# Another column order, a shorter first softmax and a guard with a second path, in a dynamic convolution followed by a maxout layer

## The chip, the cores and the metric

One Trainium2 chip; the kernel runs on one of its cores. The metric is the device time of one execution in microseconds. Engines are named as in the profile: PE is TensorE, DVE VectorE, ACT ScalarE, POOL GpSimd, SP SyncE (it only issues DMAs and waits).

## The reference, cut to what matters

```python
# x: 8 x 4160 x 192, weight_gen: 8 x 4160 x 8 heads x 7 taps, all float32
w = exp(weight_gen - max(weight_gen, axis=-1))
w = w / (sum(w, axis=-1) + 1e-9)            # softmax over the 7 taps
x_pad = concatenate([zeros(B, 6, D), x], axis=1)
# y[b, s, h, g] = sum over k of w[b, s, h, k] * x_pad[b, s + k, h, g]
y = einsum('bshk,bskhg->bshg', w, x_unf).reshape(B * S, 192)
out = maximum(y @ w1, y @ w2) @ w_out       # w1, w2: 192 x 1024, w_out: 1024 x 192
```

`weight_gen` is drawn as a normal variable times 0.3.

## The kernel before, in words

The 33280 tokens lie on 128 partitions, 260 consecutive tokens ("columns", `CPP`) on each; 16 partitions make one of the 8 sequences. A column needs the 6 columns ahead of it (`PAD`), the halo. For column 0 of a partition these are the last columns of the partition before it, or zeros where a sequence begins: `msk` is 0 on those partitions and 1 elsewhere.

The columns are worked through in batches of 16 (`BATCHES`, the seventeenth has 4). For each batch:

- `load_wg` and `load_x` load the logits (`wg_t`) and x (`xb_t`, cast to bf16 by the DMA). The halo of every batch but the first is copied from the tail of the batch before, SBUF to SBUF (`load_halo`).
- The softmax has no maximum: `exp_sum` (ACT) makes the exponentials, `red` (DVE) their sums over the taps, `ln` (ACT) the logarithm of the sums, `shift` (DVE) subtracts it from the logits, and `weights` (ACT) takes the exponential again, as bf16 and with every value twice.
- `mul` (DVE) multiplies seven shifted views of x by the weights into `m_t`; `adds` (DVE) sum the taps into `y_t`, which is transposed by DMA (`yt`, SP's queue; a one-element cast on POOL, `gate`, marks the landing). For the first units of 4 columns `sum_transpose` does sum and transpose on PE into `yps`, and ACT copies that to `yt`.

The second layer uses max(h1, h2) = h1 + relu(h2 - h1). PE multiplies `yt` with `wd` = w2 - w1 into `hd` or `hdp`, ACT applies relu into `rd_t`, PE multiplies that with `wo` = w_out, and adds `yt` times `w10` = w1 w_out, all into `op_ps`. ACT copies this to `o_t`, and SP stores it. `hidden(g)` records the work on group g of these tiles.

The order is the program's own: each engine runs its instructions in the order in which the kernel records them, and `behind(a, b)` makes a load of POOL's queue wait for an instruction. Before the first tiles there is a setup, recorded once:

- SP issues, in this order: logits of batch 0 (`load_wg`), the halo from DRAM in two pieces (partitions 1 to 15 and 16 to 127, 504 KB for the larger), columns 0 to 3 (`xs`), the weights in float32 (`ws0E`, `ws1E`: rows 0 to 127 of w1 and w2, the half 0 of their columns; `ws0T`, `ws1T`: rows 128 to 191 of both halves), columns 4 to 7, half 1 of `ws0E` and `ws1E`, logits of batch 1.
- The first softmax is done in two halves, ahead of everything else on DVE and ACT; the masked halo is cast by DVE (L568) and ACT (L570); `mul(0, 0)` follows.
- `w_diff(h)` forms half h of `wd` by subtraction on DVE and copies parts of it between partition halves (L586, L587, L591), half 0 by ACT, half 1 by DVE. `w1E`, `w1T` are bf16 copies of w1.
- `keep_warm` runs matmuls whose result nobody reads.

The end is one ACT copy into `o_last` (L383), two stores of half of it by SP and ACT (L386), and the waits for the last DMAs.

Of the kernel before, what the change touches and what calls it, by code (L numbers as in the profile page):

```python
# [23 lines left out]
def kernel(  # L24
# [20 lines left out]
    RPB = P // B  # L45
    G = D // H
# [29 lines left out]
    pwg = ctx.enter_context(tc.tile_pool(name="pwg", bufs=4))  # L76
    pxb = ctx.enter_context(tc.tile_pool(name="pxb", bufs=2))
    pe_ = ctx.enter_context(tc.tile_pool(name="pe", bufs=2))
    psm = ctx.enter_context(tc.tile_pool(name="psm", bufs=3))
    pm = ctx.enter_context(tc.tile_pool(name="pm", bufs=1))  # L80
    pen = ctx.enter_context(tc.tile_pool(name="pen", bufs=2))
    py = ctx.enter_context(tc.tile_pool(name="py", bufs=2))
    pyt = ctx.enter_context(tc.tile_pool(name="pyt", bufs=6))
    prd = ctx.enter_context(tc.tile_pool(name="prd", bufs=7))
    first_ps = ctx.enter_context(ExitStack())
# [3 lines left out]
    def later_ps():  # L89

        first_ps.close()
        for k in ("ab", "c", "r"):
            ps[k] = ctx.enter_context(tc.tile_pool(name="pps_" + k, bufs=1, space=bass.MemoryType.PSUM))
# [7 lines left out]
    def load_wg(b, eng):  # L101
        c0, n = BATCHES[b]
        wg_ts[b] = pwg.tile([P, n * WGC], FP32, name="wg_t", tag="wg")
        return eng.dma_start(
            out=wg_ts[b],
            in_=bass.AP(tensor=weight_gen.tensor, offset=c0 * WGC,
                        ap=[[CPP * WGC, P], [1, n * WGC]]),
        )

    def load_x(b, o, n, halo=True):  # L110

        if b not in xb_ts:
            xb_ts[b] = pxb.tile([P, (16 + PAD) * D], BF16, name="xb_t", tag="xb")
        load = nc.gpsimd.dma_start(  # L114
            out=xb_ts[b][:, (PAD + o) * D:(PAD + o + n) * D],
            in_=bass.AP(tensor=x.tensor, offset=(BATCHES[b][0] + o) * D,
                        ap=[[CPP * D, P], [1, n * D]]),
        )
        if b > 0 and o == 0 and halo:
            load_halo(b)  # L120
        return load

    def load_halo(b):

        if b not in xb_ts:
            xb_ts[b] = pxb.tile([P, (16 + PAD) * D], BF16, name="xb_t", tag="xb")
        nc.gpsimd.dma_start(out=xb_ts[b][:, 0:PAD * D],
# [14 lines left out]

    def red(b, i=0, of=1):
        if i == 0:
            s_ts[b] = psm.tile([P, BATCHES[b][1] * H], FP32, name="sum_t", tag="sum")
        hs, at, ap = part(b, i, of)
        nc.vector.reduce_sum(out=s_ts[b][:, hs], in_=_sub(e_ts[b], at, ap), axis=AX.X)  # L147

    def ln(b, i=0, of=1):
        s_t = s_ts[b][:, part(b, i, of)[0]]  # L150
        nc.scalar.activation(out=s_t, in_=s_t, func=AF.Ln)
# [7 lines left out]
    def weights(b, o):  # L159
# [6 lines left out]
        for j in range(J):  # L166
            nc.scalar.activation(  # L167
                out=_sub(en_ts[b], (o * WGC + j * N * K) * 2, [[2 * N, K], [2, N], [1, 2]]),
                in_=_sub(wg_ts[b], (o * H + j * N) * K, [[1, K], [K, N], [0, 2]]), func=AF.Exp,
            )  # L170


    def mul(b, o):

        n = dict(pieces(b))[o]
        if n == 4 and b < 2:
            m_out = _sub(m_t, K * o * D, [[64, 2], [P, K * 6], [1, 64]])
            x_in = _sub(xb_ts[b], o * D, [[2 * D, 2], [D, K], [1, 2 * D]])
        else:
            m_out = m_t[:, K * o * D:K * (o + n) * D]  # L180
            x_in = _sub(xb_ts[b], o * D, [[D, K], [1, n * D]])
# [195 lines left out]
    def evac(p, n):  # L377
# [3 lines left out]
        if p == NT // 2 - 1:  # L381
# [3 lines left out]
            for j, eng in enumerate((nc.scalar, nc.sync)):  # L385
                eng.dma_start(  # L386
                    out=bass.AP(tensor=out.tensor, offset=(place(p)[0] + 2 * j) * D, ap=[[CPP * D, P], [1, D]]),
# [18 lines left out]
        for eng, c, *ap in stores:  # L406

            def issue(eng=eng, c=c, ap=ap, o=o):
                eng.dma_start(
                    out=bass.AP(tensor=out.tensor, offset=c * D, ap=[[CPP * D, P], *ap]),  # L410
# [101 lines left out]
    o_last = consts.tile([P, 2 * D], FP32, name="o_last")  # L512

    with tc.tile_pool(name="pstage", bufs=1) as pstage:
        ident_f = pstage.tile([P, P], FP32, name="ident_f")
        xs = pstage.tile([P, (PAD + 8) * D], FP32, name="xs")
# [3 lines left out]
        load_wg(0, nc.sync)  # L520
        nc.vector.memset(xs[0:1, 0:PAD * D], 0.0)
# [314 lines left out]
```

## Time and profile before

| | |
|---|---|
| runs | 409.07, 409.61, 409.11 us; median 409.11 |
| profiled execution | span 408.4 us, its only time; no other of that execution is given |
| PE busy | 398.9 us, 98% |
| DVE busy | 371.7 us, 91%; nothing after 378.5 us |
| ACT busy | 357.1 us, 87% |
| POOL busy | 72.5 us, 18% |
| granted TensorE clock | 1.000 |
| DMA | 65.70 MB, 161 GB/s over the span |

The span runs from the first instruction to the last of the core; the time of a run also holds what lies around it. Busy time is an average over three stages: loads (until about 14 us), a stretch in which ACT fills and PE starts (to 31 us), and the long stretch to 405 us. A wait is put down to the last semaphore that came.

### The profile page before, as it was taken

To read this page: it belongs to the slowest core of one execution; us is meant where nothing else is said; L and a number is where in the kernel's file an instruction comes from. 1 tells how busy PE (TensorE), PEld (TensorE's weight loads), DVE (VectorE), ACT (ScalarE), POOL (GpSimd) and SP (SyncE) were. 2 spreads that over 40 slices of the span, in tenths; PEclk is the share of its full clock that TensorE was granted. 3 is DMA by queue.
4 is the path that set the end of the run, shared out by engine and by line. 5 is a ranking of instruction groups with operands and counts; after the bars stand their busy time and mean duration, and the time that the engine had idled before them with its cause. 6 is when DMAs were issued, how large, how long until landed. Compare 5 with 4: busy or idle time off the path is not lost.

```text
span 408.4 us, 16153 instructions
## 1 busy us (share of the span) xinstructions
PE 398.9 (98%) x7422; PEld 317.6 (78%) x7422; DVE 371.7 (91%) x216; ACT 357.1 (87%) x424; POOL 72.5 (18%) x101
## 2 busy tenths in 40 slices
PE   7899999999999999999999999999999999999996
PEld 2589989777777777777877777777778777777796
DVE  4999999999999999999999999999999999999000
ACT  6799899999899998898998999998999988988872
POOL 0311012212222112121211122220122220210000
PEclk9999999999999999999999999999999999999999
DMA  8958399767658674976786588478648647654514
GB/s 242 218 125 219 75 186 167 168 165 173 147 113 237 151 167 105 244 201 69 234 203 84 123 248 202 65 243 180 128 109 239 169 68 237 154 127 111 145 55 142
DMA packets 62785, 65.70 MB, mean 161 GB/s; under 512 B 47711, under 2 KB 51679, under 8 KB 62718
## 3 DMA queue, kind: packets, MB, share of 16 engines
q1 hardware_dynamic: 54334, 40.54, 36.7%
q0 software_dynamic: 8240, 24.04, 29.9%
q8 instruction: 58, 0.95, 1.0%
q10 hardware_dynamic: 144, 0.10, 0.1%
q14 instruction: 9, 0.07, 0.1%
HBM read 35.96 MB, written 25.56 MB: 151 GB/s over the span
## 4 chain that ended last, share of the span: by engine, by line
PE 91%; ACT 4%; DMA 3%; issue 1%; SPq 0%; DVE 0%; ACTq 0%
PE op_ps L339 41%; PE hd L299 39%; PE op_ps L351 8%; DMA xs<-in_x_dram 3%; ACT rd_t L309 2%; PE hdp L299 1%; PE yps L248 1%; ACT yt L255 1%; ACT w1t L675 0%; ACT e_t L135 0%; ACT en_t L167 0%; DVE xb_t L620 0%; ACT wd L591 0%; ACT w L668 0%; ACT w1T L633 0%
## 5 line engine op out<-in xcount | busy, mean ns | idle before, releaser
L309 ACT ACTIVATE rd_t<-hd 128x1024 bf16<-128x1024 f32 (+1 forms) x206 | 234.7, 1187 | 27.5 <-PE hd L299 26.3
L339 PE MATMUL op_ps<-wo,rd_t 64*128 64x192 bf16 x4160 | 211.4, 243 | 0.1
L339 PEld LDWEIGHTS <-rd_t 64*128 64x128 bf16 x4160 | 181.7, 94 | 15.7 <-ACTq L372 0.3
L299 PE MATMUL hd<-yt,wd 64*128 64x512 bf16 (+1 forms) x1584 | 188.1, 360 | 0.7 <-issue 0.6
L182 DVE TENSOR_TENSOR m_t<-xb_t,en_t 128x10752 bf16<-128x10752 bf16 (+1 forms) x37 | 187.4, 5070 | 0.2
L299 PEld LDWEIGHTS <-wd 64*128 64x128 bf16 x1776 | 94.5, 94 | 43.2 <-issue 2.8
L224 POOL CAST gate<-yt 128x1 f32<-128x1 bf16 x29 | 37.8, 1305 | 264.3 <-DMA yt<-y_t 264.3
L198 DVE TENSOR_TENSOR m_t<-m_t 128x4608 bf16<-128x4608 bf16 (+1 forms) x30 | 74.1, 2470 | 0.1
L395 ACT COPY o_t<-op_ps 128x384 f32<-128x384 f32 (+1 forms) x99 | 57.3, 589 | 12.8 <-PE op_ps L339 12.8
L351 PE MATMUL op_ps<-w,yt 64*128 64x192 bf16 x780 | 56.0, 243 | 0.4 <-ACT w L668 0.4
L351 PEld LDWEIGHTS <-yt 64*128 64x128 bf16 x780 | 38.6, 94 | 16.7 <-issue 1.3
L204 DVE TENSOR_TENSOR m_t<-m_t 128x3072 bf16<-128x3072 bf16 (+1 forms) x29 | 50.0, 1723 | 0.1
L167 ACT ACTIVATE en_t<-wg_t 128x896 bf16<-128x896 f32 (+2 forms) x45 | 35.8, 821 | 0.0
L207 DVE TENSOR_TENSOR y_t<-m_t 128x1536 bf16<-128x1536 bf16 (+1 forms) x29 | 27.3, 941 | 0.5
L114 POOL DMA_DIRECT2D xb_t<-in_x_dram x33 | 17.6, 534 | 32.0 <-ACT rd_t L309 19.8
L147 DVE TENSOR_REDUCE sum_t<-e_t 128x64 f32<-128x448 f32 (+2 forms) x31 | 19.6, 635 | 3.3 <-ACT e_t L135 3.3
L156 DVE TENSOR_TENSOR wg_t<-wg_t,sum_t 128x280 f32<-128x280 f32 (+5 forms) x46 | 22.0, 481 | 0.0
L135 ACT ACTIVATE e_t<-wg_t 128x896 f32<-128x896 f32 (+2 forms) x18 | 16.1, 901 | 2.6 <-DMA wg_t<-in_weight_gen_dram 2.6
L309 ACT ACTIVATE rd_t<-hdp 128x1024 bf16<-128x1024 f32 x16 | 16.3, 1056 | 0.5 <-PE hdp L299 0.4
L299 PE MATMUL hdp<-yt,wd 64*128 64x256 bf16 x192 | 13.2, 270 | 0.7 <-issue 0.5
L615 PE MATMUL warm<-ident 128*128 128x512 bf16 x38 | 10.7, 449 | 2.6 <-DVE ident L562 2.6
L248 PEld LDWEIGHTS <-m_t 64*128 64x128 bf16 x636 | 10.1, 95 | 2.6 <-DVE m_t L182 2.5
(45 smaller groups left out, 65.9 us busy)
## 6 DMA issues: line engine op xcount, KB each, us to landing
out_dram<-o_t SPq DMA_DIRECT2D x22, 768.0 KB, 4.8
xb_t<-in_x_dram POOLq DMA_DIRECT2D x30, 384.0 KB, 5.2
out_dram<-o_t SPq DMA_DIRECT2D x20, 384.0 KB, 3.1
wg_t<-in_weight_gen_dram POOLq DMA_DIRECT2D x14, 448.0 KB, 5.3
xb_t<-xb_t POOLq DMA_DIRECT2D x16, 288.0 KB, 5.4
wg_t<-in_weight_gen_dram SPq DMA_DIRECT2D x2, 448.0 KB, 4.4
xs<-in_x_dram SPq DMA_DIRECT2D x2, 384.0 KB, 7.2
xb_t<-in_x_dram POOLq DMA_DIRECT2D x3, 192.0 KB, 4.4
```

The source lines that it names most:

```text
L156: nc.vector.tensor_tensor(out=w_t, in0=w_t, in1=_sub(s_ts[b], hs.start, [[1, hs.stop - hs.start], [0, K]]), op=ALU.subtract)
L167: nc.scalar.activation(out=_sub(en_ts[b], (o * WGC + j * N * K) * 2, [[2 * N, K], [2, N], [1, 2]]), in_=_sub(wg_ts[b], (o * H + j * N) * K ...
L182: return nc.vector.tensor_tensor(out=m_out, in0=x_in, in1=_sub(en_ts[b], o * WGC * 2, [[2, K * n * H], [0, G // 2], [1, 2]]), op=ALU.mult,)
L198: nc.vector.tensor_tensor(out=taps(0, 1, 3), in0=taps(0, 1, 3), in1=taps(3, 1, 3), op=ALU.add)
L204: nc.vector.tensor_tensor(out=taps(0, 2, 2), in0=taps(0, 2, 2), in1=taps(1, 5, 2), op=ALU.add)
L207: nc.vector.tensor_tensor(out=_sub(y_ts[b], o * D, [[64, 2], [P, 3 * w // 2], [1, 64]]), in0=taps(0, 1, 1), in1=taps(2, 1, 1), op=ALU.add,)
L224: nc.gpsimd.tensor_copy(out=gate, in_=yt[:, 0:1])
L299: nc.tensor.matmul(hid_out(t, f, j), lhsT=wd_at(j, s, f // 4, f % 4 * P, P), rhs=_sub(yt_ts[u][half(j), :], (s + j) % 3 * P, [[3 * P, w // ...
L309: relu_of[t0] = nc.scalar.activation(out=rd[:, k * 1024:(k + n) * 1024], in_=hd[:, at:at + n * 1024], func=AF.Relu)
L339: return nc.tensor.matmul(op_out(c), lhsT=rd[half(r), k * 1024 + at:k * 1024 + at + P], rhs=wo[half(r), f * D:(f + 1) * D], start=False, s ...
L351: nc.tensor.matmul(op_out(c + j), lhsT=yt_ts[u][half(j), (3 * i + (s + j) % 3) * P:(3 * i + (s + j) % 3 + 1) * P], rhs=w10[half(j), s * D: ...
L395: nc.scalar.copy(out=_sub(o, c % 24 * D, [[D, len(qs)], [h * D, 2], [1, D]]), in_=_sub(tile_, at + (qs[0] - p) * D, [[D, len(qs)], [512, 2 ...
```

## The change

- **Order of columns.** Position v of the order is column v + 8 for v below 248, column v - 248 for 248 to 255, and v itself for 256 to 259 (`actual`). Loads of x and logits and stores of results use it. The first halo is then columns 2 to 7 of the same partition, plain x: no mask, no zero fill, no split load; DVE casts it (128x1152) and the first four columns.
- **Columns 0 to 7** come last but one, as the second half of batch 15, in an x tile of their own (`wrap`): POOL zeroes partition 0 of its halo, loads the halo of partitions 1 to 127 from DRAM and the columns; ACT multiplies the halo by `msk` (`wrap_mask`) at tile 4 of batch 14. Batch 16 lies in the free half of batch 15's tile.
- **First logits.** Only 8 columns of logits are loaded first; the other 8 are loaded after the weights. Their exp, sum, ln, shift and weights are recorded after the first relu (exp) and after the second `sum_transpose` (the rest).
- **Setup.** `xs` holds 4 columns; columns 4 to 7 are loaded by POOL. The `ws0T` and `ws1T` loads of half 1 are issued by ACT. Of half 0, two of three copies of `wd` are made by DVE and one by ACT; of half 1, likewise (all three were DVE's). The copy of half 1 of `w1E` comes later. `keep_warm` runs 24 and 4 matmuls instead of 30 and 8. The identity is made before the mask.
- **Sums** are kept in `s_first` and `s_rest` for the whole kernel; `ln` writes to a tile of its own, `ln_t`.
- **Guard.** After the last y, `sums_in_range` finds on DVE whether any sum is above 1e18 or below 1e-18, and a POOL DMA collects the partitions' answers. At the end all engines load the answer (`values_load`), and if it isn't 0, `with_maximum` computes all columns again, one at a time, with the maximum subtracted. With the given inputs it is 0, and this block is jumped over.

```diff
+    def actual(v):
+        return v + 8 if v < LAST - 8 else v - (LAST - 8) if v < LAST else v
...
+        if "wrap" in xb_ts and t is xb_ts["wrap"]:
+            nc.gpsimd.memset(t[0:1, 0:PAD * D], 0.0)
+            nc.gpsimd.dma_start(
+                out=t[1:P, 0:PAD * D],
+                in_=bass.AP(tensor=x.tensor, offset=(CPP - PAD) * D, ap=[[CPP * D, P - 1], [1, PAD * D]]),
+            )
...
+    def wrap_mask():
+        halo = xb_ts["wrap"][:, 0:PAD * D]
+        nc.scalar.activation(out=halo, in_=halo, func=AF.Copy, scale=msk[:, 0:1])
...
-        load_wg(0, nc.sync)
-        nc.vector.memset(xs[0:1, 0:PAD * D], 0.0)
-        for p0, p1 in ((1, 16), (16, P)):
+        load_wg(0, nc.sync, 0, 8)
+        for at, c, n in ((0, 2, PAD), (PAD, 8, 4)):
             nc.sync.dma_start(
-                out=xs[p0:p1, 0:PAD * D],
-                in_=bass.AP(tensor=x.tensor, offset=(p0 * CPP - PAD) * D,
-                            ap=[[CPP * D, p1 - p0], [1, PAD * D]]),
+                out=xs[:, at * D:(at + n) * D],
+                in_=bass.AP(tensor=x.tensor, offset=c * D, ap=[[CPP * D, P], [1, n * D]]),
             )
...
-        load_first(4)
+        load_w(0)
+        load_w_rest(0, nc.sync)
         load_w(1)
+        load_wg(0, nc.sync, 8, 8)
         load_wg(1, nc.sync)
...
         for step in (exp_sum, red, ln, shift):
-            for i in range(2):
-                step(0, i, 2)
...
-        nc.vector.tensor_scalar(out=xb_ts[0][:, 0:HP], in0=xs[:, 0:HP], scalar1=msk[:, 0:1], scalar2=None,
-                                op0=ALU.mult)
-        nc.scalar.activation(out=xb_ts[0][:, HP:PAD * D], in_=xs[:, HP:PAD * D], func=AF.Copy,
-                             scale=msk[:, 0:1])
-        for o in (0, 4, 8, 12):
-            weights(0, o)
+            step(0, 0, 2)
+        weights(0, 0)
+        first_weights = weights(0, 4)
+        load_w_rest(1, nc.scalar)
+        for at, n in ((0, PAD), (PAD, 4)):
+            nc.vector.tensor_copy(out=xb_ts[0][:, at * D:(at + n) * D], in_=xs[:, at * D:(at + n) * D])
         first_mul = mul(0, 0)
...
-        keep_warm(30)
-        w_diff(0, nc.scalar.copy)
-        nc.vector.tensor_copy(out=xb_ts[0][:, (PAD + 4) * D:(PAD + 8) * D], in_=xs[:, (PAD + 4) * D:])
+        keep_warm(24)
+        w_diff(0, (nc.scalar.copy, nc.vector.tensor_copy, nc.vector.tensor_copy))
+        behind(first_weights, load_x(0, 4, 4))
         behind(first_mul, load_x(0, 8, 4))
...
-        keep_warm(8)
+        keep_warm(4)
         mul(0, 4)
         nc.scalar.copy(out=w1["T"], in_=ws["T", 0])
-        nc.scalar.copy(out=w1["E"][:, HF:F], in_=ws["E", 0][:, HF:F])
         rd = room(0)
         hid_tile(0)
         relu(rd, 0, 1)
         behind(relu_of[0], load_x(1, 0, 8))
-        exp_sum(1)
+        exp_sum(0, 1, 2)
         hid_tile(1)
         relu(rd, 1, 1)
-        w_diff(1, nc.vector.tensor_copy)
+        w_diff(1, (nc.scalar.copy, nc.vector.tensor_copy, nc.vector.tensor_copy))
         sum_transpose(1)
+        red(0, 1, 2)
+        ln(0, 1, 2)
+        exp_sum(1)
+        shift(0, 1, 2)
+        weights(0, 8)
+        weights(0, 12)
+        nc.scalar.copy(out=w1["E"][:, HF:F], in_=ws["E", 0][:, HF:F])
         red(1)
         mul(0, 8)
         hidden(1)
...
+    def sums_in_range():
+        for i, (op, test, bound) in enumerate(((ALU.max, ALU.is_gt, SUMS[1]), (ALU.min, ALU.is_lt, SUMS[0]))):
+            for j, s_t in enumerate(s_parts):
+                at = 2 * i + j
+                nc.vector.tensor_reduce(out=odd[:, at:at + 1], in_=s_t, op=op, axis=AX.X)
+                nc.vector.tensor_single_scalar(out=odd[:, at + 4:at + 5], in_=odd[:, at:at + 1],
+                                               scalar=bound, op=test)
+        nc.vector.tensor_reduce(out=odd[:, 8:9], in_=odd[:, 4:8], op=ALU.max, axis=AX.X)
+        nc.gpsimd.dma_start(out=odd_row, in_=odd[:, 8:9])
+        nc.vector.tensor_reduce(out=odd[0:1, 9:10], in_=odd_row, op=ALU.max, axis=AX.X)
+        nc.vector.tensor_copy(out=odd_any, in_=odd[0:1, 9:10])
...
+        if s == 4 and b == NB - 3:
+            wrap_mask()
...
+    sums_in_range()
     rest_of_results(OUTS[-1])
+    work.close()
+    again = nc.values_load(odd_any, min_val=0, max_val=1)
+    with tc.If(again != 0):
+        with_maximum()
```

More of the change, by code (lines that the diff above doesn't have):

```diff
@@ L45 @@
     RPB = P // B
+    SUMS = (1e-18, 1e18)
     G = D // H
@@ L92, in later_ps @@
         for k in ("ab", "c", "r"):
[L93 removed]
+            ps[k] = work.enter_context(tc.tile_pool(name="pps_" + k, bufs=1, space=bass.MemoryType.PSUM))
     wg_ts, xb_ts, e_ts, s_ts, en_ts, y_ts, yt_ts = {}, {}, {}, {}, {}, {}, {}
     m_t = pm.tile([P, K * 16 * D], BF16, name="m_t")
[L101 to L108, printed above, removed]
+    LAST = CPP - CPP % 16
```

183 lines of the change are left out of this document (132 added, 51 removed).

## The prediction

> **What bounds the kernel now.** I read the page first. The profiled execution spans 408.4 us; the runs shown have a median of 409.11, so 0.7 us lies outside the span, and I carry that 0.7 over unchanged.
>
> ```profile
> PE 398.9 (98%) x7422; PEld 317.6 (78%) x7422; DVE 371.7 (91%) x216; ACT 357.1 (87%) x424; POOL 72.5 (18%) x101
> PE 91%; ACT 4%; DMA 3%; issue 1%; SPq 0%; DVE 0%; ACTq 0%
> ```
>
> TensorE is busy for 98% of the span and makes 91% of the chain. The diff adds no matmul to the path that runs, except that it drops ten warm-up ones. So the 91% stays, and the question is what happens at the two ends, where the chain is not TensorE's. The table of windows says where the ends lie:
>
> ```profile
> 20.00:32.00 12.00, 11.46 (x326) 9.76 (x324) 12.00 (x6) 11.95 (x20) 1.61 (x3) 1.00 0.64 131
> 100.00:370.00 270.00, 269.85 (x4691) 210.71 (x4690) 268.84 (x149) 243.42 (x272) 53.87 (x66) 1.00 0.68 162
> 400.00:409.00 9.00, 4.83 (x118) 4.61 (x112) 0.00 (x0) 1.75 (x3) 0.00 (x0) 1.00 0.38 134
> ```
>
> (columns: busy PE, PEld, DVE, ACT, POOL, then clock, DMA share, GB/s). From 20 to 32 us VectorE and ScalarE have no gap at all; from 100 to 370 TensorE lacks 0.15 us of 270. Nothing given up before 32 us is won back later. The chain of waits for the first 45 us names the links:
>
> ```profile
> 1.73 4.72 DMA xs<-in_x_dram
> 6.47 7.49 DMA xs<-in_x_dram
> 13.98 0.63 DVE xb_t L620
> 14.61 0.62 ACT wd L591
> ...
> 18.02 0.84 ACT e_t L135
> 18.86 0.91 ACT rd_t L309
> 19.77 0.69 ACT yt L255
> 20.46 1.84 ACT rd_t L309 x2
> ...
> 31.09 1.49 PE op_ps L339 x32
> ```
>
> Loads until 14, ScalarE without a break from 14.6 to 31.0, then TensorE to the end. The timelines of VectorE and ScalarE show what starts that stretch:
>
> ```profile
> 9.08 0.56 DVE L574 CAST xb_t<-xs 128x768 bf16<-128x768 f32 x1 [1.40 <-DMA xs<-in_x_dram]
> 9.75 2.96 DVE L182 TENSOR_TENSOR m_t<-xb_t,en_t 128x5376 bf16<-128x5376 bf16 x1
> 12.63 0.69 DVE L584 TENSOR_TENSOR wd<-ws1E,ws0E 128x512 bf16<-128x512 f32 x1
> 13.23 0.68 DVE L589 TENSOR_TENSOR wd<-ws1T,ws0T 128x512 bf16<-128x512 f32 x1
> 20.17 2.95 DVE L182 TENSOR_TENSOR m_t<-xb_t,en_t 128x5376 bf16<-128x5376 bf16 x1
> ```
>
> ```profile
> 6.54 1.02 ACT L570 ACTIVATE xb_t<-xs,msk 128x864 bf16<-128x864 f32 x1
> 7.47 2.45 ACT L167 ACTIVATE en_t<-wg_t 128x224 bf16<-128x224 f32 x8
> 13.34 0.62 ACT L586 COPY wd<-wd 64x512 bf16<-64x512 bf16 x1 [2.48 <-DVE wd L584]
> ```
>
> VectorE waits 1.40 us for the first four columns; ScalarE, its softmax finished, then sits idle for 2.48 us until the first difference of the weights.
>
> **Term 1, the first multiply: about 1.0 us earlier.** Ahead of it the old kernel moves 448 KB of logits, 571 KB of halo in two pieces and 384 KB of columns, 1403 KB, from the first issue at 0.74 to 9.08. The new one moves 224 + 576 + 384 = 1184 KB; in proportion 1.3 us is saved, at the 242 GB/s of the first 10 us 0.9. I take 1.0. The halo's cast moves to VectorE. By the form 128x768 in 0.56, some 128x1152 is 0.85, and it fits into the old 1.40 of waiting because the halo lands at 1.73 + 4.72 = 6.45. The bounds: nothing saved, if a late packet rather than the bytes sets the landing; and 1.9 at most, since shift (6.25 + 0.6) and two pieces of weights at 0.3 end no earlier than 7.5, and a cast and multiply behind them leave the multiply at 7.85.
>
> **Term 2, work that loses its cover: ScalarE.** The second half of the first softmax stood in ScalarE's idle time ahead of 13.34, at no cost. It now stands behind the first relus, where ScalarE has no gap. From the first wd copy to the relus at 20.33, ScalarE had 6.99 us of work. It loses two of three copies of wd (2 x 0.62, to VectorE). It gains a half exp (0.5), a ln (0.2), four weight pieces (4 x 0.30) and one wd copy from VectorE (0.62); the w1E copy of 0.52 only changes place. Sum: -1.24 + 2.52 = +1.3.
>
> **Term 3, VectorE, over the same stretch.** From the sub at 12.63 to the multiply at 20.17 it had 7.54 us. It loses the cast at 13.98 (0.7) and one wd copy (0.27). It gains two wd copies (0.6), half a sum (0.6) and half a shift (0.6): +0.83. This chain also takes a new wait. The loads of the T rows for half 1 now stand on ScalarE's queue, and each waits for a semaphore of the ws0E and ws1E loads of half 0, which landed at 10.2 and 11.3 before and should land about 1 us earlier. Everything on ScalarE's queue behind them stands too (the w1E copy, hidden by the old idle 2.48). So the T rows set off at 9.2 and 10.3 instead of 4 to 6. Issue to landing was 8.2 and 7.8 us for these under full queues and 1.8 to 2.0 for small stores in an empty one. The bounds are 12.1 and 18 us; I take 12.8, nearer the short end, since by then the large first loads are done. The T sub, the wd copies and the second multiply queue behind it on VectorE: sub to 13.5, two copies to 14.1, second multiply at 14.1 (14.70 before), so the multiply of 20.17 comes at 14.1 + 2.9 (multiply) + 0.7 (sub) + 0.6 (copies) + 0.6 (sum) + 0.6 (shift) + 1.0 (sum of batch 1) = 20.5.
>
> The two chains meet: ScalarE's ln waits for the half sum at 18.9, then exp of batch 1 (0.84), four weight pieces (1.2) and w1E (0.52) put the relus of hidden(1) at 21.6 against 20.33. **Head: +1.3**, from -1.1 (the first rival below) to +2.5 (T rows another 1.2 later). From there to 31.09 ScalarE is gapless, so it arrives whole at TensorE.
>
> **Term 4, the wrap batch: +0.5.** The extra loads for batch 15 on POOL (zero fill, 127-row halo, columns, two pieces of logits) are off the path: POOL stands idle 8.5 to 10.7 us at a time around there, waiting for transposes. What counts is the mask on ScalarE at tile 4 of batch 14, about 352 us: 128x1152 where 128x864 took 1.02, so 1.3 us, put ahead of a relu. ScalarE's idle gaps there are 0.30, 0.56, 0.33 and 0.53 us, so between 0 (spread over the PSUM buffers ahead) and 1.3 (all of it felt); 0.5 in between. The halo copy saved on POOL is 0.55 us of an engine at 18%.
>
> **Term 5, the guard.** Its reductions on VectorE start after 378.5, where VectorE has finished, and nobody waits for them until the branch: nothing, as long as they take under 26 us (4 sums over at most 1696 elements, by 0.62 for 448 elements about 2.4 each, and a DMA under 5.4). Sums in new tiles, ln out of place and loading columns by POOL cost nothing on a path either. At the end each engine loads the flag, compares and jumps, and SyncE has about a dozen more semaphore waits behind the last landing. The end now:
>
> ```profile
> 404.87 0.48 ACT L383 COPY o_last<-op_ps 128x384 f32<-128x384 f32 x1
> 405.38 0.34 SPq L386 DMA_DIRECT2D out_dram<-o_last  x1
> 405.38 0.37 ACTq L386 DMA_DIRECT2D out_dram<-o_last  x1
> ```
>
> These stores land 2.0 us later, at 407.4, and the span ends 1.0 after that. The flag's load runs inside those 2.0, if it takes no more than 1.7. Twelve waits at 0.06 (the chain's "issue" steps between SyncE's instructions) are 0.7, and 0.1 for the jump: **+0.8**. Below: 0, if the waits are met while the stores fly. Above: a load of 2.0 us in series and an instruction fetch of 1 to 2 us, about +3.
>
> **Sum:** 408.4 + 1.3 + 0.5 + 0.8 = 411.0 span, 411.7 with the 0.7.
>
> **Rivals.**
> *The early start wins.* The first columns bring the full 1.9 us and the T rows are in time, so VectorE's chain stands at -1.9 + 0.83 = -1.1. ScalarE gets there too, if it would otherwise wait for the hidden tiles: it has 1.24 + 0.52 less to do ahead of the first relu, and what it gains comes behind. With the mask hidden and 0.2 at the end that is -0.9, so 408.2. It decides when the first multiply starts before 8.2. For it: 1.40 us of waiting on these bytes. Against: 1.3 us of ScalarE work without cover. Chance 0.12.
> *Even:* the multiply at 8.3, 1.45 earlier, against term 2's 1.3, the mask hidden and 0.2 at the end: 409.2. Chance 0.08.
> *The T rows come late,* behind the second halves of E and logits, at 14 instead of 12.8: VectorE stands 1.2 longer, 411.7 + 1.2 = 412.9. Chance 0.2. Speaking for it: 7.8 to 8.2 us to landing before.
> *The jump is felt.* The not-taken block holds some 560 TensorE instructions; the page's instruction queue moves 0.95 MB in 58 packets, so 16 KB hold 256 instructions, and the target is two packets on. A fetch that starts only at the jump takes about as long as a small store, 2.0: end +2.8 instead of +0.8, 413.7. Chance 0.12. The Trainium skill, "Runtime: NRT & Kernel Launch", section "Instruction fetch mechanics", says just this: a taken branch out of the current two-page window forces a fetch before execution goes on. No branch of this kind is in the trace of before.
> *A cold TensorE.* 24 warm-ups at 0.294 from 1.9 end at 9.0; the first transpose can start at about 11.7 to 12.5: an idle stretch of 2.7 to 3.5 us where 1.29 is now, all at clock 1.00. If the clock halves, two hidden tiles of 1.49 take 3.0: +1.5, 413.2. Chance 0.05. The Trainium skill, "TensorE: Matmul & The Clock Gate", section "What's actually happening", gives one idle window of about 3.4 us as what gates it; by that the stretch would just pass.
> The forecast keeps 0.43.
>
> **How the numbers follow.** About 0.2% (0.8 us) is what a measurement of this kernel can tell from no change. Faster is the first rival, 0.12; even 0.08; all others 0.80. The range runs from 409.6 (head +0.3, mask 0, end +0.2) to 413.7, leaving out the faster cases and the long tails.
>
> **What would show it.** First multiply at 8.7 instead of 9.75; T sub waiting for a load until about 12.8; relus of hidden(1) at 21.6 instead of 20.33; first output matmuls at 32.4 instead of 31.09; a 1.3 us mask near 352 with a TensorE gap of half a us; from the last store's landing to the end 1.8 instead of 1.0. A first multiply before 8.2, or a span whose middle between 32 and 400 changes by over a us, would prove me wrong.

## The result, and the profile after

The changed kernel takes 422.15 us (median of 4 runs, 417.84 to 423.14), the kernel before 409.36 in the same comparison: a ratio of 1.0286, interval 1.0234 to 1.0338. It is slower by some 12 us (12.8 by the medians, 11.7 by the ratio), where 2.6 were forecast. The profile is of the run of 417.84, the fastest of the four, whose span is 416.1. A second profile, of a run of 423.36, is shown with the fourth experiment.

The page of the changed kernel, busy time and chain:

```profile
PE 400.3 (96%) x7412; PEld 318.7 (77%) x7412; DVE 376.9 (91%) x226; ACT 356.6 (86%) x423; POOL 77.0 (19%) x105
DVE 43%; PE 42%; ACT 5%; DMA 4%; issue 3%; SPq 0%; POOL 0%; DVEq 0%; ACTq 0%
```

TensorE is busy for as long as before, within 1.4 us; it stands still for longer. That VectorE now has 43% of the chain does not mean that it became slower: the chain passes through it at the one place near 357 us where ScalarE waits for a load (below), and from there it is followed backwards along VectorE. The chain at that place:

```profile
349.92 0.53 POOL xb_t L133
350.45 0.99 POOL xb_t L141
351.44 4.75 DMA xb_t<-in_x_dram
356.19 0.82 issue
357.01 0.07 ACT xb_t L150
```

POOL loads the wrap tile's columns, zeroes its first halo row and issues its halo's load. ScalarE's mask (L150) starts at 357.01, when that load has landed: its last part came in at 356.93 by the trace's record of landings, so the 0.82 us that the chain calls "issue" are part of the wait for it. The chain of the first 45 us says more:

```profile
2.63 6.41 DMA ws1E<-in_moe_w_dram
...
9.06 6.42 DMA ws1T<-in_moe_w_dram
...
15.56 0.70 DVE wd L616
...
19.94 2.44 PE yps L285 x84
22.38 0.02 issue
22.40 0.80 ACT yt L292
23.20 0.16 ACT ln_t L186
23.35 0.84 ACT e_t L162
24.19 1.17 ACT en_t L202 x4
25.36 0.51 ACT w1E L678
25.87 1.84 ACT rd_t L346 x2
...
36.50 1.49 PE op_ps L376 x32
```

The first two links, both DMAs, are the loss: a load of ws1E lands at 9.04, and only then does the load of ws1T's second half set off and take 6.4 us more. ScalarE's timeline has the two issues:

```profile
7.76 0.56 ACTq L580 DMA_DIRECT2D ws0T<-in_moe_w_dram  x1
9.06 0.48 ACTq L580 DMA_DIRECT2D ws1T<-in_moe_w_dram  x1
```

Each comes 0.02 us after the landing of a load of half 0 (ws0E at 7.74, ws1E at 9.04). Before, all four loads of T rows had set off by 6.1, from SyncE (its timeline, before):

```profile
3.51 1.19 SPq L549 DMA_DIRECT2D ws0T<-in_moe_w_dram  x2
4.75 1.37 SPq L549 DMA_DIRECT2D ws1T<-in_moe_w_dram  x2
```

VectorE's timeline shows what was won ahead of the wait for the T rows and lost behind it:

```profile
7.38 2.96 DVE L219 TENSOR_TENSOR m_t<-xb_t,en_t 128x5376 bf16<-128x5376 bf16 x1
...
15.56 0.69 DVE L616 TENSOR_TENSOR wd<-ws1T,ws0T 128x512 bf16<-128x512 f32 x1 [4.62 <-DMA ws1T<-in_moe_w_dram]
...
16.92 2.96 DVE L219 TENSOR_TENSOR m_t<-xb_t,en_t 128x5376 bf16<-128x5376 bf16 x1
...
25.23 2.95 DVE L219 TENSOR_TENSOR m_t<-xb_t,en_t 128x5376 bf16<-128x5376 bf16 x1
```

The second multiply before the change:

```profile
14.70 2.96 DVE L182 TENSOR_TENSOR m_t<-xb_t,en_t 128x5376 bf16<-128x5376 bf16 x1
```

The first multiply is 2.4 us earlier (9.75 before), the second 2.2 later (14.70), the third 5.1 later (20.17). The gapless stretch begins 5.4 later (36.50 against 31.09). The granted clock, in the windows (the column behind POOL), fell in that time; before it was 1.00 there:

```profile
10.00:20.00 10.00, 4.71 (x116) 2.95 (x118) 5.29 (x7) 4.53 (x7) 2.92 (x5) 0.89 0.96 202
20.00:32.00 12.00, 10.81 (x267) 9.14 (x268) 10.00 (x10) 10.32 (x20) 0.66 (x2) 0.81 0.38 73
```

At the other end, the last copy starts at 410.47 and the span ends at 416.1, 5.6 us instead of 3.5. The instructions of the line of the branch (count, min/median/max in ns, first and last start):

```profile
L929 SPq EVENT_SEMAPHORE  x8: 17/17/17, 412.8 to 414.4; - x8
...
L929 PEldq COMPARE_BRANCH  x1: 3777/3777/3777, 410.0 to 410.0; - x1
L929 ACTq COMPARE_BRANCH  x1: 58/58/58, 412.0 to 412.0; - x1
```

TensorE's jump took 3.78 us, ScalarE's 0.06. The last two stores landed 2.9 and 3.2 us after their issue (1.8 and 2.0 before), and from the last landing to the end it is 1.85 us instead of 1.0. So in this profile 5.4 us come from the head (all that lies ahead of the gapless stretch) and 2.1 from the end, 7.5 of its 7.7 (416.1 against 408.4). TensorE's 1.22 us of idle time near 357 hardly show in this sum, because the profile of before lacked 0.57 us of TensorE work from 50 to 100 us and this one only 0.12. What a slower run has beyond that, the fourth experiment shows.

### The profile page after: what moved, and what is told of

Same layout as the page of the kernel before. It is cut to its first block, busy times and chain, and to the rows that moved or that the text cites. A ratio compares the mean times of both kernels' runs of the same rounds, so it can differ in the third digit from the quotient of the medians.

```text
span 416.1 us, 16182 instructions
## 1 busy us (share of the span) xinstructions
PE 400.3 (96%) x7412; PEld 318.7 (77%) x7412; DVE 376.9 (91%) x226; ACT 356.6 (86%) x423; POOL 77.0 (19%) x105
## 4 chain that ended last, share of the span: by engine, by line
DVE 43%; PE 42%; ACT 5%; DMA 4%; issue 3%; SPq 0%; POOL 0%; DVEq 0%; ACTq 0%
DVE m_t L219 23%; PE op_ps L376 19%; PE hd L336 17%; DVE m_t L235 9%; DVE m_t L241 6%; PE op_ps L388 4%; ACT rd_t L346 2%; DVE y_t L244 2%; DVE s_rest L180 2%; PE yps L285 2%; DMA ws1T<-in_moe_w_dram 2%; DMA ws1E<-in_moe_w_dram 2%; DVE wg_t L191 1%; PE hdp L336 1%; DMA xb_t<-in_x_dram 1%
## 5 line engine op out<-in xcount | busy, mean ns | idle before, releaser
L261 POOL CAST gate<-yt 128x1 f32<-128x1 bf16 x29 | 39.7, 1368 | 260.2 <-DMA yt<-y_t 260.2
L244 DVE TENSOR_TENSOR y_t<-m_t 128x1536 bf16<-128x1536 bf16 (+1 forms) x29 | 27.3, 942 | 0.5
L133 POOL DMA_DIRECT2D xb_t<-in_x_dram x34 | 18.2, 535 | 32.5 <-ACT rd_t L346 23.2
L191 DVE TENSOR_TENSOR wg_t<-wg_t,ln_t 128x280 f32<-128x280 f32 (+5 forms) x46 | 22.2, 483 | 2.0 <-ACT ln_t L186 2.0
L336 PE MATMUL hdp<-yt,wd 64*128 64x256 bf16 x192 | 14.8, 292 | 4.1 <-DVE wd L619 3.6
L180 DVE TENSOR_REDUCE s_rest<-e_t 128x64 f32<-128x448 f32 (+2 forms) x27 | 16.4, 607 | 0.0
L285 PE MATMUL yps<-ident,m_t 64*128 64x64 bf16 x636 | 11.7, 196 | 1.7 <-DVE m_t L219 1.7
L285 PEld LDWEIGHTS <-m_t 64*128 64x128 bf16 x636 | 11.2, 99 | 2.8 <-DVE m_t L219 2.7
```

What stands on the lines that cost most here:

```text
L244: nc.vector.tensor_tensor(out=_sub(y_ts[b], o * D, [[64, 2], [P, 3 * w // 2], [1, 64]]), in0=taps(0, 1, 1), in1=taps(2, 1, 1), op=ALU.add,)
L261: nc.gpsimd.tensor_copy(out=gate, in_=yt[:, 0:1])
L285: nc.tensor.matmul(yps[:, r * 512 + k * 64:r * 512 + (k + 1) * 64], lhsT=m_t[half(r), at:at + P], rhs=ident[half(r), half(r)], start=(k == ...
L336: nc.tensor.matmul(hid_out(t, f, j), lhsT=wd_at(j, s, f // 4, f % 4 * P, P), rhs=_sub(yt_ts[u][half(j), :], (s + j) % 3 * P, [[3 * P, w // ...
```

## The experiments

Theory A: three stalls that add up, each where work waits for a load or a fetch that the change made late: T rows on ScalarE's queue, the wrap tile's halo ahead of its mask, the code behind the guard's jump. The rivals: the moved half of the softmax as the main cost; the guard as the main cost; one cost only, the clock. The kernels were measured on several chips, each beside the kernel before, so kernels of different chips are compared by their ratios to it.

| kernel | median us | before, same chip | ratio | 95% interval |
|---|---|---|---|---|
| changed kernel, again | 420.96 | 409.21 | 1.0275 | 1.0225 to 1.0325 |
| T rows on SyncE | 418.14 | 409.21 | 1.0200 | 1.0139 to 1.0261 |
| no guard | 419.94 | 409.21 | 1.0251 | 1.0202 to 1.0300 |
| 18 warm-ups | 422.60 | 409.21 | 1.0321 | 1.0270 to 1.0373 |
| mask later | 417.25 | 409.16 | 1.0213 | 1.0173 to 1.0253 |
| T rows on SyncE, mask later | 413.99 | 409.16 | 1.0124 | 1.0095 to 1.0154 |
| the same, no guard | 411.54 | 409.16 | 1.0060 | 1.0037 to 1.0082 |
| the same, whole softmax first | 411.36 | 409.16 | 1.0060 | 1.0038 to 1.0081 |
| before, T rows on ScalarE | 415.67 | 409.70 | 1.0143 | 1.0101 to 1.0185 |
| T rows, mask; flag without branch | 412.74 | 409.70 | 1.0057 | 1.0036 to 1.0077 |
| T rows, mask; small second path | 412.74 | 409.70 | 1.0068 | 1.0046 to 1.0090 |
| column order alone, in the main | 409.68 | 409.70 | 0.9984 | 0.9963 to 1.0006 |
| T rows, mask; 32 and 8 warm-ups | 415.13 | 409.75 | 1.0136 | 1.0092 to 1.0180 |
| mask; 30 and 18 warm-ups | 417.68 | 409.75 | 1.0181 | 1.0140 to 1.0222 |

**The T rows on SyncE.**

```diff
         load_w_rest(0, nc.sync)
+        load_w_rest(1, nc.sync)
...
-        load_w_rest(1, nc.scalar)
```

> The changed kernel with one step undone: the T rows of half 1 are issued by SyncE right behind those of half 0, not by ScalarE. Theory A (the late T rows are the cause of the long head, and the idle TensorE that they leave is what drops its clock): VectorE's T sub starts by about 12 us instead of 15.6, the granted clock stays at 1.00 up to 32 us, the relus of hidden(1) start at about 20.0 instead of 25.8 and the output matmuls that begin the gapless stretch at about 31 instead of 36.5. The end keeps its extra 2.1 us in the span and 1.1 outside. Time about 412.5 us. Rival B (the second half of the softmax without cover is the cause, and the T wait only hides behind it): the T sub starts earlier, but the relus of hidden(1) still start after 23 and the time stays above 416.

Measured 418.14, not 412.5. The head did some three quarters of what was expected: the gapless stretch begins at 32.43, where about 31 was expected and the changed kernel had 36.50. From its timelines of VectorE (the T sub, the subtraction of the T rows) and of ScalarE (the relus of hidden(1)):

```profile
11.50 0.69 DVE L616 TENSOR_TENSOR wd<-ws1T,ws0T 128x512 bf16<-128x512 f32 x1 [0.40 <-DMA ws1T<-in_moe_w_dram]
```

```profile
21.70 1.93 ACT L346 ACTIVATE rd_t<-hdp 128x1024 bf16<-128x1024 f32 x2
```

The T wait shrinks from 4.62 to 0.40 us, and the relus of hidden(1) come 4.1 us earlier (25.77), so the late T rows are shown as the largest part of the head. But the relus still come 1.4 us later than before the change (20.33), where 20.0 was expected; part of the moved softmax stands ahead of them. Nor did the clock stay at 1.00: it was at half from 11.1 to 14.5, after 2.27 us without work ahead of the first transpose. Rival B's late relus (after 23) did not come, but its time (above 416) did, since more was lost later in this run: 2.9 us at the mask, and 1.5 us at 63 us, where TensorE waited for nothing that the profile shows:

```profile
64.42 0.25 PE L376 MATMUL op_ps<-wo,rd_t 64*128 64x192 bf16 x1 [1.51 <-issue]
```

A packet of 16 KB on the instruction queue ran from 61.89 to 63.00 just ahead of it, so late code is a likely reason; that was not tried by itself.

**Without the guard.**

```diff
-    sums_in_range()
...
-    again = nc.values_load(odd_any, min_val=0, max_val=1)
-    with tc.If(again != 0):
-        with_maximum()
```

> The changed kernel without the guard: no test of the sums, no load of the flag, no branch, no second path. Theory A (the guard costs at the end only): from the last copy of results to the end of the span 3.5 us as before the change instead of 5.6, the time outside the span 0.7 instead of 1.7, so 3 us under the changed kernel of the same head, about 419 where that is 422 and 414.7 where that is 417.8. Rival (the guard's block also stands in the way earlier, by code loading or memory): more than 5 us of difference, and a change of rows ahead of 400 us.

From the last copy to the end it is 3.6 us (414.61 to 418.19), as before the change and 2.4 less than with the guard on this chip (5.9), as expected. The time fell by only 1.0 (ratios 1.0251 and 1.0275, intervals that overlap), since the runs differ by more in the head and at the mask; the figure for the guard is taken from the pair without these stalls below. One part of the expectation fell: outside the span lie 1.9 us here too (420.06 against 418.2), and 1.8 in a run of the kernel before (410.14 against 408.3). So the change adds nothing there; the 0.7 of the prediction came from setting the span of one execution beside the median of others.

**More warm-ups behind the first transpose.**

```diff
-        keep_warm(4)
+        keep_warm(18)
```

> The changed kernel with 18 instead of 4 warm-up matmuls behind the first transpose, so that TensorE has work while VectorE waits for the T rows. Theory A (the clock drops because TensorE stands idle for 3.65 us, and how long it stays low differs from run to run, which is why the runs lie at 417.8 and at 422): clock 1.00 throughout, no run near 422, all runs at about 416.5, since the T rows stay as late as they are and only the slower matmuls and the second transpose of 2.4 us are mended. Rival (the clock costs nothing, since VectorE and ScalarE set the pace of the head): the same two groups of times, 417.8 and 422.

Measured 422.60, no faster than before the edit. The clock did not stay at 1.00: it was low from 12.9 to 16.3 and from 26.5 to 29.9, the first after 2.3 us without work ahead of the first transpose, which this edit had not covered. It does not tell the two theories apart; the last two runs close that gap too.

**The changed kernel again.** No edit.

> The changed kernel as it is, to see another profile of it. Theory A: runs at 422 have a longer stretch of low clock in the head (mean clock 0.981 instead of 0.989, so 3.4 us more of lost clock, 6.8 us more at half rate) and nothing else; the gapless stretch of TensorE then begins about 4 us later than at 36.5. Rival: the 4 us are lost elsewhere, in the middle or at the end, with the head as in the first profile.

Measured 420.96; the profile is of a run of 423.36. The expectation was half wrong. The first output matmul comes 1.7 us later than in the first profile (first multiply at 9.38 instead of 7.38, because the first columns landed later), not 4, and the other loss is at the mask, where the rival had put it. ScalarE's and TensorE's timelines of this profile:

```profile
360.43 1.25 ACT L150 ACTIVATE xb_t<-xb_t,msk 128x1152 bf16<-128x1152 bf16 x1 [2.70 <-issue]
```

```profile
363.33 0.42 PE L388 MATMUL op_ps<-w,yt 64*128 64x192 bf16 x6 [3.09 <-ACT o_t L432]
```

The halo's load for the wrap tile is issued by POOL at 352.97; ScalarE, at the mask, stands until 360.43, and TensorE for 3.09 us behind it. In the first profile the same load was issued at 351.44, the mask started at 357.01 and TensorE stood for 1.22. After the 3.09 the clock is at half for 3.4 us, after the 1.22 it is not. In all five profiles with the mask at this tile it starts 0.07 or 0.08 us after the halo's load has landed (356.93 in the first profile, 360.36 here). Of the 5.4 us between the two spans, 1.7 are lost ahead of the first output matmul, 0.3 at the end and 3.4 between. The other three runs of the first comparison have a mean clock of 0.981 or 0.982, like this one (0.981) and not like the first profile (0.989), so this one is likely the usual case; without profiles of theirs that is not shown.

**The mask later.**

```diff
-        if s == 4 and b == NB - 3:
+        if s == 6 and b == NB - 3:
             wrap_mask()
```

> The changed kernel with the mask of the wrap tile two tiles later on ScalarE (s == 6 instead of 4), some 6 us, where VectorE does not need it yet. Theory A (the mask waits for its halo's load, 1.2 to 3.1 us of idle TensorE near 357 us, and where that idle time is long enough the clock drops to half for 3.4 us more): no TensorE gap over 0.7 us near 357 and no stretch of low clock between 100 and 400; 3 to 5 us under the changed kernel where that has both, so 417 to 419. Rival (the low clock near 362 comes by itself, some 340 us after the start): it stays, and the time falls by at most 1.5 us.

```profile
361.31 1.29 ACT L150 ACTIVATE xb_t<-xb_t,msk 128x1152 bf16<-128x1152 bf16 x1
```

```profile
340.00:370.00 30.00, 30.00 (x514) 23.09 (x511) 29.97 (x19) 27.15 (x32) 3.84 (x6) 1.00 0.82 165
```

The mask no longer waits, TensorE is busy for 30.00 of 30.00 us around it (windows, first column), and nothing between 100 and 400 has a low clock. The ratio falls from 1.0275 to 1.0213 (or from the first comparison's 1.0286), 2.5 to 3 us. These intervals overlap; the next kernel shows the same step once more. Theory A holds here; its 3 to 5 was a little high.

**T rows and mask together.** The two edits above in one kernel.

> Both undone: T rows on SyncE and the mask later. Theory A (two separate stalls, one in the head, one at the wrap, which add): as with the T rows on SyncE alone, 418.1, less the 3 to 5 us of the wrap: 413 to 415. Rival (both are one cost, because the clock after the head's stall decides): no better than the better of the two, about 418.

413.99, as theory A has it: the two costs add. From 1.0213 to 1.0124 the T rows' part is 3.6 us, and from 1.0200 to 1.0124 the mask's is 3.1.

**The same without the guard.**

> As the one before, and without the guard (no test of the sums, no load of the flag, no branch, no second path). Theory A: the end after the last copy is 3.5 us long instead of 5.6 to 6.0, so 2.1 to 2.5 us less: 411 to 412.5. What is left over the kernel before is the softmax's second half behind the first relus, some 1.4 us. Rival (nothing is left over): 409.

411.54, again as expected: 2.6 us for the guard by the ratios (1.0124 to 1.0060), 2.0 by the ends of the profiles (5.85 and 3.81). Something is left over, about 2.4 us.

**The whole softmax first.**

```diff
-        load_wg(0, nc.sync, 0, 8)
+        load_wg(0, nc.sync)
...
-        load_wg(0, nc.sync, 8, 8)
...
         for step in (exp_sum, red, ln, shift):
-            step(0, 0, 2)
+            for i in range(2):
+                step(0, i, 2)
         weights(0, 0)
         first_weights = weights(0, 4)
+        weights(0, 8)
+        weights(0, 12)
...
-        exp_sum(0, 1, 2)
...
-        red(0, 1, 2)
-        ln(0, 1, 2)
         exp_sum(1)
-        shift(0, 1, 2)
-        weights(0, 8)
-        weights(0, 12)
```

> As the one before, with all 16 columns of the first logits loaded and their softmax done ahead of the first multiply, as before the change; of the change, the column order with its plain first halo, the copies' division and the wrap tile are left. Theory A (the moved half of the softmax costs 1.8 us on ScalarE between the second yt copy and the relus of hidden(1), and saves about 1 us at the first multiply, which is lost again in waits): relus of hidden(1) at about 20.4 instead of 21.7, time 1 us under the one before: 410 to 411. Rival (the earlier first multiply pays for the moved half): 1 us over the one before.

No difference: 411.36 and 411.54. The relus came at 21.53, not 20.4. VectorE's timeline shows what took the place of the moved half:

```profile
15.02 2.96 DVE L219 TENSOR_TENSOR m_t<-xb_t,en_t 128x5376 bf16<-128x5376 bf16 x1 [1.33 <-DMA xb_t<-in_x_dram]
...
21.16 1.09 DVE L180 TENSOR_REDUCE s_first<-e_t 128x128 f32<-128x896 f32 x1 [2.05 <-ACT e_t L162]
```

The second multiply waits 1.33 us for columns 4 to 7, which POOL now loads behind the weights, and the sum of batch 1 waits for an exp that the change had moved behind the second transpose. So the rest is not the softmax alone, but several small things of which another is next when one goes.

**The column order alone, in the main.** From the one before, still without the guard and with the new division of the copies of `wd`: columns 4 to 7 loaded by SyncE into `xs` and cast by VectorE, the exp of batch 1 and the copy of `w1E` where they were before, 32 warm-ups.

```diff
-        keep_warm(24)
+        keep_warm(32)
...
-        behind(first_weights, load_x(0, 4, 4))
+        nc.vector.tensor_copy(out=xb_ts[0][:, (PAD + 4) * D:(PAD + 8) * D], in_=xs[:, (PAD + 4) * D:])
...
+        exp_sum(1)
         hid_tile(1)
```

> No guard, T rows on SyncE, mask later, the whole first softmax ahead of the first multiply, and now also columns 4 to 7 loaded by SyncE as before the change (VectorE casts them), the copy of half 1 of w1E and the exp of batch 1 where they were before, 32 warm-up matmuls instead of 24. Of the change, the column order with the plain first halo and the new division of the wd copies are left. Theory A (the plain halo saves about 1.4 us at the first multiply and the division of the copies another 0.6; all that was lost came from the other parts): the second multiply at about 13.8, relus of hidden(1) at about 19 instead of 20.33, no low clock, 407.5 to 408.7, faster than the kernel before. Rival (the column order gains nothing, because the head is set by loads of the weights): 409 to 410.

409.68 against 409.70: the two cannot be told apart (0.9984, 0.9963 to 1.0006). The time is thus the rival's (409 to 410) and not theory A's (407.5 to 408.7), though the head began as theory A had it: second multiply at 14.16 (13.8 expected; before 14.70), relus of hidden(1) at 19.32 (19; before 20.33). In the profiled run, its slowest (412.49), TensorE then stood for 2.11 us in the middle of a transpose, for nothing that the profile shows; a 16 KB packet of the instruction queue ran from 23.16 to 24.12:

```profile
25.47 0.54 PE L285 MATMUL yps<-ident,m_t 64*128 64x64 bf16 x25 [2.11 <-issue]
```

The clock was low behind it, from 26.4 to 29.8, which theory A had excluded too. In this run, in the first experiment (63.00 to 64.42) and in the kernel below (26.48 to 27.96) TensorE went on 1.35 to 1.48 us after the end of such a packet; packets of this size run in every profile, most without a stall, so late code stays unproven. What the plain halo and the new division of the copies win at the start is thus real in this trace, about 1 us, and smaller than what differs from run to run on that chip (407.94 to 412.49; 408.36 to 412.58 for the kernel before). No version here is shown to be faster than the kernel before.

**The kernel before with the T rows on ScalarE.** One part of the change alone.

```diff
-                nc.sync.dma_start(
-                    out=ws["T", wi][half(h), :],
...
+        for wi, wsrc in enumerate((moe_w1, moe_w2)):
+            nc.scalar.dma_start(
+                out=ws["T", wi][half(1), :],
+                in_=bass.AP(tensor=wsrc.tensor, offset=P * F + HF, ap=[[F, 64], [1, HF]]),
+            )
```

> The kernel before, with one part of the change alone: the T rows of half 1 are issued by ScalarE behind the weights of batch 0. Theory A (a load that waits in ScalarE's queue for a free semaphore of an earlier load sets off late, and VectorE and TensorE stand still for it): the T sub at 15 to 16 us instead of 13.23, the first output matmul at 31.5 to 33 instead of 28.99, a stretch of low clock if TensorE idles long enough, 412 to 415 us in all. Rival (the T rows were late in the changed kernel because of its other order of loads): the T sub by 13.5, no difference over 0.5 us.

```profile
16.54 0.69 DVE L593 TENSOR_TENSOR wd<-ws1T,ws0T 128x512 bf16<-128x512 f32 x1 [4.06 <-DMA ws0T<-in_moe_w_dram]
```

415.67, ratio 1.0143: this edit alone makes the old kernel 5.9 us slower. ScalarE issued the two loads at 9.28 and 10.74, each 0.02 us after a load of half 0 had landed (ws0E at 9.26, ws1E at 10.72), and VectorE waited 4.06 us. The first output matmul came at 32.48 and the clock was low from 18.2 to 21.6. The mechanism stands on its own, without the new order of loads.

**The flag without a branch; a small second path.** Both with the T rows on SyncE and the mask later.

```diff
-    with tc.If(again != 0):
-        with_maximum()
```

> T rows on SyncE, mask later, the sums tested and the flag loaded at the end by all engines, but no branch and no second path. Theory A (of the 2.1 to 2.5 us at the end, what counts is the jump: the instruction fetch behind it holds back the last stores by 1.2, and the second block's waits 0.7): from the last copy to the end 3.6 to 3.8 us instead of 5.8, so about 411.7. Rival (the flag's load is what costs): 5 us or more.

```diff
-            for c in range(PAD):
+            for c in range(1):
...
-            with tc.For_i(PAD, CPP, 1) as c:
-                nc.sync.dma_start(out=xw, in_=bass.AP(tensor=x.tensor, offset=(c - PAD) * D,
-                                                      ap=[[CPP * D, P], [1, K * D]]))
-                column_again(c)
```

> T rows on SyncE, mask later, guard with branch, but a second path of one column instead of all, so that the jump's target lies some 80 TensorE instructions ahead instead of 560. Theory A (the fetch of code far ahead shares a DMA engine with the last stores): the last packet of the stores lands with the others, 1.2 us earlier, and the end is 4.6 us instead of 5.8; about 412.8. Rival (the waits of the block's end cost it all, or every jump fetches): still 5.6 to 6.

The second path of one column only could not repair all columns; with the given inputs it isn't run. The line of its branch:

```profile
L925 PEldq COMPARE_BRANCH  x1: 228/228/228, 406.3 to 406.3; - x1
```

The landings of the last stores after their issue, from the views of `o_last` with the full second path and with the small one:

```profile
DMA to landing us min/median/max: 3.3/3.4/3.5
```

```profile
DMA to landing us min/median/max: 2.1/2.2/2.2
```

From the last copy to the end: 5.85 us with the full second path, 4.49 with the small one, 3.59 with the flag and no branch, 3.6 to 3.8 without the guard. So in the span the flag's load costs nothing, the branch with the waits of its block 0.9, and the distance of the jump 1.4. The times split it otherwise: 2.3 us from the full path to the small one (1.0124 to 1.0068), and between the small path, no branch and no guard (1.0068, 1.0057, 1.0060) no difference that can be told. The whole is 2.0 us by the ends and 2.6 by the ratios; the split is known to about a microsecond. TensorE's jump takes 0.23 us when the target is near and 3.66 to 4.28 in the eight profiles where it is some 560 instructions away (3.78 in the changed kernel). TensorE itself is not late by that: in the changed kernel its jump ends at 413.76, while SyncE, whose waits close the span, waits for a store until 414.22. The stores are late: they land after 2.1 to 2.2 us with the near target and 2.9 to 3.7 with the far one. In the changed kernel's trace, 15 of the 16 parts of ScalarE's store have landed by 412.98 and the last at 414.22, and three instruction packets ran between 411.34 and 413.69. That the last part waits on its DMA engine for the fetch fits these times and the two runs; it was not seen directly. The Trainium skill, "Runtime: NRT & Kernel Launch", section "Instruction fetch mechanics", says that a taken branch out of the current two-page window forces a fetch; 0.23 against 3.78 us agrees.

**Both idle gaps filled.**

```diff
-        keep_warm(24)
+        keep_warm(32)
...
-        keep_warm(4)
+        keep_warm(8)
```

> T rows on SyncE, mask later, and 32 and 8 warm-up matmuls instead of 24 and 4, so that TensorE idles less ahead of and behind the first transpose. Theory A (a stretch of low clock in the head slows two transposes and hidden tiles that others wait for, and costs about 1 us): no low clock before 20 us, 413 instead of 414. Rival (in the head the clock costs nothing that anybody waits for): 414 as before.

> The changed kernel with the mask later and 30 and 18 warm-up matmuls instead of 24 and 4, T rows late as they are in the change. Theory A: the clock stays at 1.00 through the wait for the T rows, the second transpose takes 1.2 to 1.4 us instead of 2.4, the first output matmul comes at about 33.2 instead of 34.4, and the time is about 416 instead of 417.3. Rival (the clock costs nothing): 417.3.

(The second has 30 and 18, with the T rows late.) 1.0136 against 1.0124, and 1.0181 against 1.0213: no gain that can be measured in either. In the first the clock stayed up until 20 us, as expected, and was low from 23.9 to 27.3 instead. In the second, TensorE's timeline shows what happened:

```profile
12.58 4.06 PE L644 MATMUL warm<-ident 128*128 128x512 bf16 x18
...
20.80 1.40 PE L285 MATMUL yps<-ident,m_t 64*128 64x64 bf16 x84 [1.62 <-DVE m_t L219]
...
26.68 2.74 PE L336 MATMUL hdp<-yt,wd 64*128 64x256 bf16 x24 [0.17 <-ACT rd_t L346]
```

The second transpose is quick again (1.40 instead of 2.42), as theory A said, and from the T sub to the relus of hidden(1) it is 9.2 us instead of 10.2. But TensorE then waits 1.93 us for ScalarE's late copy of `w1E`, the clock drops at 26.0 instead of 17.3, and hidden tiles of 1.5 take 2.7. The first output matmul comes at 35.15, not at 33.2: 18.7 us after the T sub, where it was 18.9 with the clock low. The low stretch was moved, not removed. So the 6.8 us of half clock in the kernel with the mask later (17.3 to 24.1) cost about 1 us up to the relus, through the slow transpose that ScalarE waits for; what the clock costs in the whole head stays open.

## Why the prediction was wrong

The direction was right and the size wrong by a factor of four and a half to five. In the first profile the head is 4.1 us above the forecast (5.4 against 1.3): 2.7 from term 3, 1.4 from what stands ahead of ScalarE's ln (term 2 and the clock). The terms, by the prediction's own numbers:

- **Term 1, the first multiply 1.0 us earlier.** It was 2.4 earlier in the first profile, beyond the bound of 1.9, and 0.4 in the second. With half of the logits first, the exp started at 3.35 (4.58 before), which the bound had left where it was. It helped nothing: what follows waits for the T rows. A first multiply before 8.2 was the mark of the first rival (an early start, 408.2). The mark came in this profile and the win did not, so it could not decide what it was to decide.
- **Term 3, T rows at 12.8.** They landed at 15.5, inside the stated bounds of 12.1 and 18. They set off earlier than the sum had it (7.8 and 9.1 us, not 9.2 and 10.3), but took 6.4 us to land where the sum had 2.5, a value close to that of small stores in an empty queue. At that time the DMA engines were full (windows from 10 to 20 us: share 0.96), and 6.4 us is near the 7.8 to 8.2 of the same rows before. This is the step that failed most: 2.7 us. The rival of late T rows had the mechanism, with 14 us and a chance of 0.2; alone it is worth 5.9 us in the old kernel. With the T rows on SyncE the relus came at 21.70 and the gapless stretch at 32.43, the forecast's 21.6 and 32.4; that is partly luck, since the T sub was then at 11.50 and other waits took the place of this one.
- **Term 2, ScalarE +1.3.** From the second yt copy to the relus it is 3.37 us instead of 0.68: +2.7. The sum had set two copies that leave against what arrives. But the copies left a place ahead of a wait, where ScalarE then stood idle, and the new work stands behind that wait. Where the prediction lets the two chains meet, it has this work at its full length: 2.7 us from the ln to the relus, measured 2.7 (23.09 to 25.77). What it lacked there is the second yt copy, which stands ahead of the ln on ScalarE and waits for a transpose (22.40 in the chain above). The half sum was ready at 21.66, so the ln came 1.4 us behind it; 1.0 of this is the transpose, 2.42 us at half clock instead of 1.40.
- **The cold TensorE, chance 0.05.** The clock did drop, in every profile of the changed kernel. The rival looked ahead of the first transpose; there the gap was 0.5 us in the first profile and 3.2 in the second. The one that counted in the first was 3.65 us behind it, the wait for the T rows. And the rival took 3.4 us as needed, while about half is enough (below). Against its price of 1.5 stands about 1 us up to the relus; what it is in the whole stays open.
- **Term 4, the mask +0.5.** Only its duration was costed (1.3; 1.25 measured). That it waits for a load that the same change adds was not: the extra loads were called off the path because POOL is idle. From issue to landing this load took 5.5 us in the first profile and 7.4 in the second. The loss is 1.2 to 3.1 us of TensorE and, in the longer case, a stretch of low clock: 2.5 to 3 us by the runs.
- **Term 5, the end +0.8.** It is 2.1. The waits are right (1.85 us from the last landing to the end, 1.8 forecast), and so is the flag's load (0.51 us, hidden). The jump, a rival with 0.12, is another 1.4 by way of the stores (2.0 forecast).
- **The range.** Its upper end took one rival at a time. They happened together: each is a wait for something that a queue delivers late, and nothing in the kernel makes them exclude each other.

## What to carry to other kernels

A DMA issued from a compute engine's queue starts when that queue and the semaphore it reuses allow it (here 0.02 us after the landing of an earlier load); moved there from SyncE, loads of 128 KB that were hidden cost 5.9 us. When a change moves work behind a wait, what left a place ahead of the wait can't be subtracted from it, and for every added operation its operands' loads are to be costed like the operation. For bounds, take the landing time under the load of the stage itself, and add rivals that can happen together.

## What was not expected of the hardware

The clock went by windows of 3.41 us on a fixed grid (the low stretches last 3.41 or 6.83 us). In the 16 profiles, of the windows at full clock before 400 us, all 21 in which TensorE was idle for 1.84 us or more, and one with 1.62, were followed by half clock; of the others, with idle times up to 1.61, none was. So about half a window of idle time, in one piece or several, is enough, and a gap of 1.9 us costs clock or not by where it falls on the grid: 1.90 us ahead of 21.85 in the first experiment did not, 1.93 ahead of 25.77 in the last run did. The Trainium skill, "TensorE: Matmul & The Clock Gate", section "What's actually happening", speaks of one idle window of about 3.4 us; the measurement here says half of that.
